# The first tile of v loaded by SyncE's queue behind f instead of by GpSimd's queue behind q and k of the second quad

## The chip, the cores and the metric

The kernel runs on one core of a Trainium2 chip. The metric is the device time of one execution in microseconds (us); the times of a kernel are given as the median of its runs. Profiles are of one execution each and have a time of their own.

## What is computed

The reference is causal attention with a forgetting decay, followed by an MLP with tanh-GELU. There are 8 batches of 8 heads, 576 positions and 64 columns per head; the MLP has 4608 tokens (8 x 576), a width of 512 and a hidden width of 2048. All inputs and the output are float32.

```python
log_f = np.log(np.clip(f, 0.0001, 1.0))
cum = np.cumsum(log_f, axis=-1)
scores = q @ k.T / sqrt(64) + cum[..., :, None] - cum[..., None, :]
attn = softmax(where(causal, scores, -1e9))
x = (attn @ v), heads side by side          # 4608 x 512
out = gelu_tanh(x @ w_in) @ w_out           # 4608 x 512
```

## The kernel before

The 64 heads are worked through as 16 quads of 4 heads (two quads per batch), and the 4608 tokens of the MLP as 9 chunks of 512. Per quad, k and q arrive as float32 and are cast to bf16 by the DMA (`load_one`, L204, issued from GpSimd, called POOL here), are transposed in 32x32 words by VectorE (DVE, L212) into kT and qT, and TensorE (PE) makes the scores (L275). ScalarE (ACT) takes their exponential into pt (L283), POOL or DVE set the part above the diagonal to zero (L289, L319). The decay does not enter the scores: as exp(cum_i - cum_j) falls apart into two factors, the key's factor wT = exp(-cum - 64) is multiplied into v (`make_vw`, L229, giving vw), and the query's factor cancels in the division by the denominator. The denominators are products of pt with w_bf, the bf16 copy of wT (L690, L691); the attention output is a product of pt with vw (L331 in the first two quads, L345 after), divided on its way into xT (L377). The MLP's first product (L414 for the first chunk, L390 and L463 after), GELU (L421, L398, L476) and second product (L609 for the first chunk, L542 after) follow, in part by a scheme with seven products for eight.

v comes per batch in five tiles of up to 128 positions, each for 8 heads: a tile is 128 x 8 x 64 float32, 256 KB, in runs of 64 values (L183). `load_v` takes the issuing engine as an argument. The word LP loads a tile of batch 0 by POOL's queue, LU the same by SyncE's (SP's) queue, LC and LX tiles of batch 1 by POOL's, LV and LB those of later batches by SP's.

The order of the work on every engine is the order in which it is written down: `setup()` and then tables of words, each word a function and its arguments (`ops`, L696; `run`, L747). A word such as `TK.0` issues its instructions on their engines at that place; engines then go on by themselves and wait for each other through semaphores. So POOL's DMA issues stand in one line with its memsets, masks and products. Two things hold back a DMA issue: data that it overwrites, and a semaphore that it shares with the eighth DMA before it from the same kind of queue, whose landing it waits for.

Around the change the order is this. In `setup()`, SP issues f; POOL issues k and q of quad 0, makes the identity, issues k and q of quad 1, makes the triangle. DVE clears buffers and clips f; ACT takes its logarithm; PE transposes it (L642). Then the words of SETUP: in the kernel before `TK.0` (DVE transposes k of quad 0) and `LP.0 LP.1` (POOL issues v tiles 0 and 1 of batch 0). After them the table FRONT begins:

```
Z TQ.0 LP.2 TR WI.1 TQ.1 S.0.0 B.1.384 CW WI.0 TK.1 S.0.2 LP.4 LP.3 B.2.256 vw.0.0 B.4.256 H.1.0.1 ...
```

Z are memsets on POOL (L649 to L652); TQ.0, TQ.1 and TK.1 the other transposes; WI pieces of w_in by POOL's queue; S.0.0 the scores of quad 0 for its first 256 positions; B matmuls that only keep PE busy (L254); CW the matmuls of the cumulated decay (L661, L663) with the exponential into wT (L666); `vw.0.0` the first use of v: DVE multiplies tiles 0 and 1, four heads, by wT (L229). `H.1.0.1` are scores of quad 1. Later words of FRONT, all on POOL, are q and k of quad 2, the rest of w_in, four pieces of w_out (WO, L199, 512 KB each) and the tiles of batch 1. The first chunk's second product (L609) needs all four pieces of w_out.

Of the kernel before, what the change touches and what calls it, by code (L numbers as in the profile page):

```python
# [16 lines left out]
def kernel(  # L17
# [51 lines left out]
    ON_ACT = ()  # L69

    SETUP = """
        TK.0 LP.0 LP.1
    """

    FRONT = """
# [723 lines left out]
```

## Time and profile before

| What | Value |
|---|---|
| Median of 3 runs | 326.88 us (326.15 to 329.17) |
| The profiled execution, its own time | 327.29 us |
| Span of its profile, first to last instruction | 325.6 us |
| DVE, ACT, POOL busy | 232.9, 207.3, 106.2 us |
| POOL's DMA queue (q0): packets, MB | 9632, 15.99 |
| SP's DMA queue (q1): packets, MB | 37664, 16.60 |
| HBM read, written | 36.85 MB, 9.44 MB |

The profile is read thus. PE is TensorE's matmuls, PEld its weight loads, which lie beside the matmuls. Lines such as L229 are lines of the kernel. "out<-in" names the tiles written and read. Idle time in square brackets is that of the engine just ahead of the instruction, with what ended it; "issue" is time in which the profile shows no releaser. A DMA's time to landing runs from its issue to the semaphore that tells of it. q0 is the queue of POOL (software_dynamic), q1 that of SP (hardware_dynamic); the core's 16 DMA engines serve both, and a share is the time that a queue's packets took, as a share of 16 engines' time, which can be over 100% as packets overlap. The small packets of 4 bytes, counted as "under 512 B" beside larger ones in q0, carry no data.

### The profile page before, as it was taken

To read this page: it belongs to the slowest core of one execution; us is meant where nothing else is said; L and a number is where in the kernel's file an instruction comes from. 1 tells how busy PE (TensorE), PEld (TensorE's weight loads), DVE (VectorE), ACT (ScalarE), POOL (GpSimd) and SP (SyncE) were. 2 spreads that over 40 slices of the span, in tenths; PEclk is the share of its full clock that TensorE was granted. 3 is DMA by queue.
4 is the path that set the end of the run, shared out by engine and by line. 5 is a ranking of instruction groups with operands and counts; after the bars stand their busy time and mean duration, and the time that the engine had idled before them with its cause. 6 is when DMAs were issued, how large, how long until landed. Compare 5 with 4: busy or idle time off the path is not lost.

```text
span 325.6 us, 12168 instructions
## 1 busy us (share of the span) xinstructions
PE 312.2 (96%) x5514; PEld 217.5 (67%) x5514; DVE 232.9 (72%) x374; ACT 207.3 (64%) x252; POOL 106.2 (33%) x145
## 2 busy tenths in 40 slices
PE   0999989999999999999999999999999999999996
PEld 0656834454777567766778887657765777588785
DVE  4665208898989886797769776778665865498674
ACT  4685656875856776579558765876668742746510
POOL 8879316442111215530643144403450150000000
PEclk9999999999999999999999999999999999999999
DMA  7999999586125961296119711761020102010212
GB/s 126 234 170 164 207 238 215 126 166 120 34 40 118 238 128 54 67 201 109 52 45 200 132 54 36 171 97 52 14 92 0 34 6 99 0 34 0 99 35 97
DMA packets 47492, 33.44 MB, mean 103 GB/s; under 512 B 29776, under 2 KB 42192, under 8 KB 47440
## 3 DMA queue, kind: packets, MB, share of 16 engines
q0 software_dynamic: 9632, 15.99, 28.4%
q1 hardware_dynamic: 37664, 16.60, 19.6%
q8 instruction: 43, 0.70, 0.9%
q10 hardware_dynamic: 144, 0.07, 0.1%
q14 instruction: 9, 0.07, 0.1%
HBM read 36.85 MB, written 9.44 MB: 142 GB/s over the span
## 4 chain that ended last, share of the span: by engine, by line
PE 83%; DMA 6%; POOL 5%; ACT 2%; DVE 1%; issue 1%; POOLq 0%; DVEq 0%
PE ps_w L542 29%; PE ps_h L390 25%; PE po L345 9%; PE ps_u L463 8%; PE ps_s L275 7%; DMA w_out_sb<-in_moe_w_out_dram 4%; PE pso L609 4%; ACT pt L283 2%; DMA q_c<-in_q_dram 2%; POOL pt L289 1%; POOL vw L229 1%; POOL w_out_sb L199 1%; POOL v_nat L183 1%; POOL w_in_sb L195 1%; PE cum_ps L663 1%
## 5 line engine op out<-in xcount | busy, mean ns | idle before, releaser
L283 ACT ACTIVATE pt<-ps_s 128x1024 bf16<-128x1024 f32 (+2 forms) x100 | 93.8, 988 | 48.8 <-PE ps_s L275 45.6
L390 PE MATMUL ps_h<-xT,w_in_sb 128*128 128x512 bf16 (+1 forms) x416 | 84.8, 354 | 0.1
L289 POOL TENSOR_SCALAR_AFFINE_SELECT pt<-pt 128x512 bf16<-128x512 bf16 (+3 forms) x65 | 39.7, 622 | 108.8 <-ACT pt L283 108.0
L390 PEld LDWEIGHTS <-w_in_sb 128*128 128x128 bf16 x416 | 40.6, 98 | 33.6 <-issue 0.4
L398 ACT ACTIVATE gT<-ps_h 128x1024 bf16<-128x1024 f32 x44 | 44.8, 1017 | 21.9 <-PE ps_h L390 21.6
L542 PEld LDWEIGHTS <-gT 128*32 128x32 bf16 (+1 forms) x1354 | 45.0, 97 | 3.8 <-issue 0.4
L542 PE MATMUL ps_w<-w_out_sb,gT 128*32 128x256 bf16 (+1 forms) x954 | 41.8, 273 | 0.0
L275 PE MATMUL ps_s<-qT,kT 32*128 32x64 bf16 (+5 forms) x896 | 36.6, 263 | 3.3 <-DVE qT L212 3.0
L542 PEld LDWEIGHTS <-gsum 128*32 128x32 bf16 (+1 forms) x1026 | 35.6, 97 | 3.0 <-issue 1.3
L229 POOL TENSOR_TENSOR vw<-v_nat,wT 128x1280 bf16<-128x1280 f32 (+1 forms) x13 | 29.4, 2262 | 11.4 <-DMA v_nat<-in_v_dram 11.4
L275 PEld LDWEIGHTS <-kT 32*128 32x128 bf16 x896 | 16.9, 93 | 19.5 <-issue 11.8
L542 PE MATMUL ps_w<-usum,gsum 128*32 128x256 bf16 (+1 forms) x791 | 29.3, 273 | 0.0
L377 DVE TENSOR_TENSOR xT<-po,rb 128x576 bf16<-128x576 f32 x26 | 19.7, 756 | 10.8 <-PE po L345 10.1
L559 DVE COPY snap<-ps_w 128x512 f32<-128x512 f32 x32 | 21.7, 677 | 6.7 <-PE ps_w L542 6.7
L479 DVE TENSOR_TENSOR usnap<-ps_u,usnap 128x512 f32<-128x512 f32 x27 | 17.8, 685 | 10.4 <-PE ps_u L463 6.1
L212 DVE STREAM_TRANSPOSE kT<-k_c 128x576 f32<-128x576 f32 x16 | 20.0, 1247 | 5.0 <-DMA k_c<-in_k_dram 5.0
L345 PE MATMUL po<-pt,vw 128*32 128x64 bf16 (+4 forms) x624 | 22.5, 279 | 0.0
L520 DVE TENSOR_TENSOR gsum<-gT 128x1024 bf16<-128x1024 bf16 x14 | 11.0, 785 | 14.8 <-ACT gT L476 12.7
L212 DVE STREAM_TRANSPOSE qT<-q_c 128x576 f32<-128x576 f32 x16 | 19.9, 1244 | 2.3 <-DMA q_c<-in_q_dram 2.1
L345 PEld LDWEIGHTS <-vw 128*32 128x32 bf16 x672 | 14.4, 97 | 10.4 <-issue 3.7
L206 POOL DMA_DIRECT2D k_c<-in_k_dram x16 | 9.1, 569 | 28.3 <-DVE kT L212 11.6
L476 ACT ACTIVATE gT<-usnap 128x512 bf16<-128x512 f32 x18 | 11.1, 630 | 9.5 <-DVE usnap L479 9.5
(113 smaller groups left out, 431.5 us busy)
## 6 DMA issues: line engine op xcount, KB each, us to landing
out_dram<-o_st SPq DMA_DIRECT2D x35, 256.0 KB, 2.3
k_c<-in_k_dram POOLq DMA_DIRECT2D x16, 288.0 KB, 5.5
q_c<-in_q_dram POOLq DMA_DIRECT2D x16, 288.0 KB, 5.9
v_nat<-in_v_dram SPq DMA_DIRECT2D x16, 256.0 KB, 4.6
v_nat<-in_v_dram SPq DMA_DIRECT2D x20, 128.0 KB, 3.9
v_nat<-in_v_dram POOLq DMA_DIRECT2D x8, 256.0 KB, 8.4
w_in_sb<-in_moe_w_in_dram POOLq DMA_DIRECT2D x8, 256.0 KB, 7.8
w_out_sb<-in_moe_w_out_dram POOLq DMA_DIRECT2D x4, 512.0 KB, 11.9
```

The source lines that it names most:

```text
L212: return nc.vector.transpose(out=dst.rearrange("p s c -> p (s c)").bitcast(FP32) .rearrange("p (t a) -> p a t", a=S // 32), in_=src.rearra ...
L229: return eng.tensor_mul(vw[i % 2][:, t0:t1], vb[:, t0:t1, h0:h0 + 4, :], wT[:, i, t0:t1, :].unsqueeze(3).to_broadcast([128, t1 - t0, 4, D]))
L275: nc.tensor.matmul(tiles[h // 2][:, h % 2, c0:c0 + nq], key_columns(i, key, h, c), qq[32 * h:32 * h + 32, q0:q0 + nq, c], start=(c == 0 an ...
L283: nc.scalar.activation(p[:, 2 * g:2 * g + 2, off:off + n], t[:, :, 0:n], AF.Exp, scale=scale)
L289: nc.gpsimd.affine_select(out=x, in_=x, compare_op=ALU.is_ge, fill=0.0, base=0, pattern=pattern, channel_multiplier=-1)
L345: nc.tensor.matmul(po[r0:r0 + w.shape[-1], 448 + q0:448 + q0 + nq], w, p[:, h, col:col + nq], start=(key in (0, "low")), stop=(key in ("lo ...
L377: nc.vector.tensor_mul(xT[:, 2 * u + x, r0 + s0:r0 + s1], po, rbs[i, part])
L390: nc.tensor.matmul(ph[:, j, n * cols:(n + 1) * cols], w_in_sb[:, dt, 128 * ft:128 * ft + 128], xT[:, dt, h0:h0 + cols], start=(dt == 0 and ...
L398: nc.scalar.activation(gelus(c, 2 * pr, 2), ph, AF.Gelu_apprx_tanh)
L463: nc.tensor.matmul(ps[:, n, :], w[:, d, 128 * n:128 * n + 128], x[:, d, :], start=(first and n == 0 and d == 0), stop=(d == 1), skip_group ...
L542: nc.tensor.matmul(ps[c0:c0 + width, n, cols[0]:cols[1]], x[:, j, 128 * n + c0:128 * n + c0 + width], w[:, j, cols[0]:cols[1]], start=(fir ...
L559: copy(kept[name], ps)
```

## The change

In SETUP the word `LP.0` is gone from behind `TK.0`, and `LU.0` stands ahead of it. Both words load the same tile: v of batch 0, positions 0 to 127, all 8 heads, into the first tile of v_nat0.

```diff
     SETUP = """
-        TK.0 LP.0 LP.1
+        LU.0 TK.0 LP.1
     """
```

The two words differ only in the engine that issues the DMA:

```python
"LU": lambda t: load_v(0, ts=(t,)),                    # eng=nc.sync
"LP": lambda t: load_v(0, ts=(t,), eng=nc.gpsimd),
```

In the order of the instructions by engine, SP has one DMA more, directly behind that of f and ahead of its first output; POOL has one fewer, the first of its two v tiles behind q and k of quad 1. PE, DVE and ACT have the same instructions in the same order.

## The prediction

> **What bounds the kernel now.** I read, in this order, the page's busy shares, the chain of waits that ended last, the timeline of the first 62 us, and the DMA view of short windows.
>
> ```profile
> span 325.6 us, 12168 instructions
> ...
> PE 312.2 (96%) x5514; PEld 217.5 (67%) x5514; DVE 232.9 (72%) x374; ACT 207.3 (64%) x252; POOL 106.2 (33%) x145
> ```
>
> TensorE (PE) is busy for 312.2 of 325.6 us. So a change can gain or lose only in the 13.4 us in which PE is idle, or by lengthening them. By the timeline 7.9 of these lie before 8.65 us (4.91 before the first matmul at 4.91, 2.97 before L275). After 46.2 us the list of PE's waits for other work adds up to 0.9 us, of which 0.6 is the wait that ends at 46.13. So the first 46 us decide. The chain of waits in that stretch (start, length, what):
>
> ```profile
> 2.02 5.29 DMA q_c<-in_q_dram
> ...
> 8.65 0.83 PE ps_s L275 x14
> ...
> 31.97 14.11 DMA w_out_sb<-in_moe_w_out_dram
> 46.09 0.04 issue
> 46.13 1.67 PE pso L609 x7
> ```
>
> The reader is to see two transfers on it: q of quad 0, which lands at 7.31 and lets DVE make qT and PE start its scores at 8.65; and the last quarter of w_out, which lands at 46.08. The timeline has the waits that matter here (start, duration, engine, line, then idle time and releaser):
>
> ```profile
> 11.32 1.26 DVE L212 STREAM_TRANSPOSE qT<-q_c 128x576 f32<-128x576 f32 x1 [1.95 <-DMA q_c<-in_q_dram]
> ...
> 13.84 0.09 PEld L275 LDWEIGHTS <-kT 32*128 32x128 bf16 x1 [0.21 <-DVE kT L212]
> ...
> 42.90 1.02 PE L609 MATMUL pso<-w_out_sb,gT 128*128 128x512 bf16 x4 [0.63 <-DMA w_out_sb<-in_moe_w_out_dram]
> ...
> 46.13 1.67 PE L609 MATMUL pso<-w_out_sb,gT 128*128 128x512 bf16 x7 [0.61 <-DMA w_out_sb<-in_moe_w_out_dram]
> ```
>
> First: q of quad 1 is awaited by DVE for 1.95 us and, through its transposes, by PE for 0.21. Last: PE waits for w_out 0.63 and 0.61, together 1.24 us. A PE that comes to 42 us later, while w_out lands as before, finds these waits shorter. No row shows PE or DVE waiting for the first tile of v.
>
> **The change part by part.** The edit takes one DMA (256 KB, L183) out of GpSimd's (POOL's) queue, where it is the fifth, and puts it second into SP's. The order of the instructions on PE, DVE and ACT is the same in both programs.
>
> *POOL.* The removed issue is half of the "x2" group at 4.70 (1.82 us), so 0.91 us. What follows moves up by 0.91: the memsets of L649 from 6.56 to 5.65, the next v tile from 8.19 to 7.28, the first two w_in pieces from 9.10 to 8.19. POOL's next wait for ACT with idle time is L289 at 17.24 (1.84 idle), so the lead ends there and is no gain by itself. Each POOL DMA waits for the landing of the eighth before it; with one DMA gone the pairs from the thirteenth on are the same as before. The four pairs ahead of that (two w_in pieces, two v tiles) wait for a transfer one place earlier, which lands sooner. Cost nothing.
>
> *SP.* The new issue stands behind f's (0.58 us at 0.81) and ahead of nothing until SP's first output at 47.91. f's own packets are ahead of v's; f lands at 3.6 and its use, cum_ps at 9.70, has over 3 us of slack. Cost nothing.
>
> *The 16 DMA engines.* Here is the price. v's packets now run while k and q of quad 0 are under way. I price this by rows of the same two queues in the steady part, where SP's queue brings v tiles beside POOL's q and k:
>
> ```profile
> q0 software_dynamic: 527, 1.10, 95.8%
> q1 hardware_dynamic: 608, 0.15, 16.1%
> ```
> ```profile
> q0 software_dynamic: 200, 0.43, 108.6%
> ```
>
> The columns are packets, MB and share of 16 engines. The first fence is the window 112 to 118 us, both queues full: 527 packets of q0 in 6 us are 88 per us, beside 1.15 packets of v for each of q0. The second is 46 to 48, q0 alone: 100 per us. So company costs q0 14%. One v packet takes 16.1% x 6 us x 16 / 608 = 25 ns of an engine. In the window 3 to 6.3 q0 has 266 packets and 103% of the engines, almost all of k and q of quad 0. 14% of 3.3 us is 0.45 us: q lands at 7.76, and L275 starts at 9.1. Lower end: the windows 2 to 3 and 3 to 4 have the engines at 0.72 and 0.91, so 0.37 us could take v for nothing, which leaves 0.1. Upper end: all of v served first. From 109 to 110 us, with q1 alone, 1039 such packets passed in 1 us, so v's 1024 take 1.0; the far row is 52 to 58 us, with outputs too, where q0 made 349 packets in 6 us, 58 per us, which would make 3.3 us into 5.7, +2.4. I take 0.45: the row 112 to 118 has the same two kinds of transfer and no stores. Nothing is gained at q's landing, since no packet that went ahead of it is removed.
>
> [...] The windows show 1.15 to 1, so I keep the row.
>
> *The second quad.* Per engine k and q of both quads are 32 packets; beside them go 32 x 1.15 = 37 of v, 37 x 25 ns = 0.9 us. So q of quad 1 and the transposes at 11.32 and 12.42 come up to 0.9 later, kT at 14.55 instead of 13.65. PE, itself 0.45 late, could absorb about 0.2 (it goes on at 14.10 where kT had come at 13.65 and the weight load at 13.84), so its scores of quad 1 are late by 0.7. ACT, which runs without a gap from 13.36 to 22.36, gets a gap of 0.3 there. I carry 0.7; ends 0.1 and 1.3.
>
> *v itself.* The tile landed 7.8 us after 4.70, at 12.5, and the next at 13.6, just before L229 used both at 13.71 (wT, its other input, came at 13.46). Now the second is first in POOL's queue and lands near 12.6. The first has 27 of 64 packets per engine left when q of quad 1 is through; it lands near 13 to 14. L229 waits for kT until 14.55 anyway, so cost nothing. If that cover is gone, the casts of L690 behind it are late next; they ended at 15.04 and the first product that reads w_bf began at 16.24, so the first 1.2 us are free.
>
> *From 14 to 46 us.* PE is busy without a gap over 0.2 until 31.3, so 0.7 arrives there in full. The w_out pieces decide what is left of it. POOL's issues after 17.24 follow ACT, so they move by 0.7 too. But transfers are late by less if the engines have a backlog:
>
> ```profile
> q0 software_dynamic: 196, 0.18, 74.3%
> ```
> ```profile
> DMA packets 126, 0.21 MB, mean 141 GB/s; under 512 B 7, under 2 KB 56, under 8 KB 126
> ```
>
> The first is 19.5 to 21 us: engines run dry, for the next issue (q, 19.78) came late. The second is 21 to 22.5: 56 - 7 = 49 packets of w_in are still moving, so the slowest engines had not run dry when the new packets came, and a transfer has landed only when its last engine is done. From 23 to 46 the queue's share is 112%. So w_out is late by something between -0.9 (the tile's 256 KB gone from ahead of it at the 285 GB/s of 9 to 11 us) and +0.7 (POOL's delay in full). I take +0.2: near zero for the backlog, above it for the 74.3%.
>
> *Sum.* PE reaches 42.27 0.7 late; its two waits for w_out shrink by 0.7 - 0.2 = 0.5 of their 1.24; 0.2 us is left. Nothing after 46.2 gives or takes. The profiled execution took 327.29 us (span 325.6 and 1.69 around it), 0.41 above the median of the three runs, 326.88. So 327.5 for that execution, and 327.1 for the median. Its own range is -0.2 to +0.7: 326.7 to 327.6.
>
> **The rivals.**
>
> *Nothing is absorbed.* w_out is late by as much as PE, for POOL's issues hang on ACT. For it: POOL waits for ACT at 17.24 and again at 24.65 (0.94 idle). Against: 49 packets of backlog. +0.7 to +1.3: 327.6 to 328.2.
>
> *v goes first, and it is slower.* Place: the engines from 3 us on. Price: 1.0 us at q's landing, up to 2.4 by the row 52 to 58. For it: from 111 to 112, when q0 began beside a full q1, q0 passed 21 packets and q1 425. Against: 112 to 118. It decides from the point where q's delay is over the 1.24 us that the w_out waits can take up, or where these move along; +1.1 to +2.1: 328.0 to 329.0. [...]
>
> *w_out lands earlier, and it is faster.* The engines use the half-empty time at 2 to 4 us for v, and 256 KB fewer stand ahead of w_out. Then both waits of 1.24 go, less what PE is late: -0.5, and -1.2 if q is not late at all: 325.7 to 326.4. Against: 103% and 112% shares leave little empty time, and POOL's later issues wait for ACT.
>
> That v comes too late for L229 is within the second rival's sum. That the change does nothing to any transfer is within my own range.
>
> **How the numbers follow.** Chances: absorbed 0.45, nothing absorbed 0.25, v first 0.12, earlier w_out 0.18. The likeliest gives 327.1. The range leaves out the far half of the faster case and the end of the slower one, and allows for a median of few runs where three runs of one kernel spread from 326.15 to 329.17: 326.0 to 328.8. About 1% (3.3 us) is what a measurement of this kernel can tell from no change. Faster by that much would need more than all of PE's waits at w_out: 0.01. Slower by that much needs 3.3 us at q's landing, or v first at the far row's price with nothing absorbed and more: 0.03. Within 1%: 0.96.
>
> **What would show it.** In the changed kernel's timeline: the POOL group at 4.70 is one issue and L649 starts near 5.65; the first qT starts near 7.8 instead of 7.33 and L275 near 9.1; the second qT near 12.0; L229 on DVE near 14.5 with no wait for v; L609's waits for w_out together near 0.7 instead of 1.24, the last ending near 46.3. I am wrong if L275 starts after 10 (v went first), at 8.65 (company is free), if L229 waits for v, or if the last w_out wait ends before 45.8 or after 46.9.

## The result and the profile after

| | Kernel before | Changed kernel |
|---|---|---|
| Median, 22 runs each | 326.81 us (325.48 to 329.17) | 327.94 us (326.98 to 330.22) |
| Ratio to before, 95% interval | | 1.0032 (1.0018 to 1.0046) |
| The profiled execution | 327.29 us | 328.84 us |
| Span | 325.6 us | 327.1 us |

The changed kernel is slower by 1.13 us, 0.3%: less than the 1% that a few runs can tell, but with 22 runs the interval lies above 1. (A ratio is recorded with its interval for each comparison; it is not the quotient of the two medians.) Its page begins as follows.

```profile
span 327.1 us, 12153 instructions
...
PE 312.1 (95%) x5499; PEld 217.8 (67%) x5514; DVE 233.5 (71%) x374; ACT 207.3 (63%) x252; POOL 104.8 (32%) x144
```

PE's busy time over the whole span is the same (312.1 against 312.2 us), but this profile has 15 matmul records fewer (5499 against 5514), most of them late in the span. What counts here is the stretch up to the end of PE's last wait for w_out, at 46.13 in the kernel before and at 47.36 in the changed one. One row for each (stretch, its length, then busy time and instructions of PE, PEld, DVE, ACT and POOL, granted clock, DMA share, GB/s):

```profile
0.00:46.13 46.13, 36.01 (x473) 24.91 (x474) 21.33 (x46) 29.21 (x36) 31.07 (x53) 1.00 1.05 189
```
```profile
0.00:47.36 47.36, 36.87 (x471) 25.34 (x473) 20.88 (x46) 29.24 (x36) 30.22 (x52) 1.00 1.00 184
```

Of the 1.23 us by which this moment is later, PE is busy for 0.86 and idle for 0.37: its matmuls take longer, and it also waits longer. The chain of waits in the first 60 us (start, length, what) shows where the first part comes in and what it has become at 47 us:

```profile
2.03 6.21 DMA q_c<-in_q_dram
...
9.57 0.83 PE ps_s L275 x13
...
11.90 2.35 PE cum_ps L663 x8
...
33.55 13.77 DMA w_out_sb<-in_moe_w_out_dram
47.32 0.04 issue
47.36 1.67 PE pso L609 x7
```

q of quad 0 lands 6.21 us after its issue instead of 5.29, and PE starts at 9.57 instead of 8.65. The eight matmuls of L663, which are no different, then take 2.35 us instead of 1.79. The last piece of w_out is used at 47.36 instead of 46.13. The same steps in the timeline of the changed kernel (start, duration, engine, line; idle time and releaser last):

```profile
8.26 1.26 DVE L212 STREAM_TRANSPOSE qT<-q_c 128x576 f32<-128x576 f32 x1 [0.42 <-DMA q_c<-in_q_dram]
...
11.36 1.26 DVE L212 STREAM_TRANSPOSE qT<-q_c 128x576 f32<-128x576 f32 x1 [1.37 <-DMA q_c<-in_q_dram]
...
14.79 0.69 DVE L229 TENSOR_TENSOR vw<-v_nat,wT 128x512 bf16<-128x512 f32 x1 [1.10 <-ACT wT L666]
14.84 1.24 PE L254 MATMUL idle_ps<-idle 128*128 128x256 bf16 x6
...
16.01 0.97 PE L275 MATMUL ps_s<-qT,kT 32*128 32x256 bf16 x16
...
19.08 1.22 POOL L289 TENSOR_SCALAR_AFFINE_SELECT pt<-pt 128x512 bf16<-128x512 bf16 x2 [4.38 <-ACT pt L283]
...
21.60 0.57 POOL L206 DMA_DIRECT2D q_c<-in_q_dram  x1
...
44.10 1.02 PE L609 MATMUL pso<-w_out_sb,gT 128*128 128x512 bf16 x4 [0.74 <-DMA w_out_sb<-in_moe_w_out_dram]
...
47.36 1.67 PE L609 MATMUL pso<-w_out_sb,gT 128*128 128x512 bf16 x7 [0.64 <-DMA w_out_sb<-in_moe_w_out_dram]
```

The reader is to see the lateness grow to 1.91 us and arrive at w_out as 1.23: q's transpose at 8.26 (before 7.33, +0.93); the scores of quad 1 at 16.01 (before 14.10, +1.91); POOL, which has 4.38 us idle for ACT where it had 1.84, issues q of quad 2 at 21.60 (before 19.78, +1.82); and PE's two waits for w_out are 0.74 and 0.64, no shorter than before (0.63 and 0.61). The 0.68 made up between 16.01 and 47.36 is not made up there; 0.57 of it is idle time ahead of L414 at 31.86 in the kernel before, which is gone in the changed one. q of quad 1 (11.36, before 11.32) is not late, and DVE's use of v waits for wT and not for v.

What the DMA engines do at the start is in the DMA view, with packets, MB and share of 16 engines. First the window 3 to 4 us, the kernel before, then the changed one.

```profile
q0 software_dynamic: 57, 0.13, 91.5%
```
```profile
q1 hardware_dynamic: 259, 0.07, 28.6%
q0 software_dynamic: 14, 0.03, 27.8%
```

While v's 256-byte packets pass, POOL's queue gets 14 packets through where it had 57, and both queues together fill only 56% of the engines' time: here POOL's queue hardly starts, and not because the engines are full. Then the window 5 to 6 us, in the same order.

```profile
q0 software_dynamic: 97, 0.20, 110.7%
```
```profile
q1 hardware_dynamic: 392, 0.10, 48.5%
q0 software_dynamic: 63, 0.11, 63.3%
```

Here the two queues together are at 112%, and POOL's queue loses packets to v all the same: 63 instead of 97, with 6.2 of v for each. Over 2 to 6 us POOL's queue passes 149 packets instead of 257; 56 of these 108 are lost before 4 us, 52 after it. So q's transfer is late both because it hardly starts and because it shares full engines later.

### The profile page after: what moved, and what is told of

Its sections match the earlier page's. It is cut to its first block, busy times and chain, and to the rows that moved or that the text cites. A ratio compares the mean times of both kernels' runs of the same rounds, so it can differ in the third digit from the quotient of the medians.

```text
span 327.1 us, 12153 instructions
## 1 busy us (share of the span) xinstructions
PE 312.1 (95%) x5499; PEld 217.8 (67%) x5514; DVE 233.5 (71%) x374; ACT 207.3 (63%) x252; POOL 104.8 (32%) x144
## 4 chain that ended last, share of the span: by engine, by line
PE 81%; DMA 6%; POOL 5%; DVE 3%; issue 2%; ACT 2%; POOLq 0%; DVEq 0%
PE ps_w L542 29%; PE ps_h L390 23%; PE po L345 9%; PE ps_u L463 8%; PE ps_s L275 8%; DMA w_out_sb<-in_moe_w_out_dram 4%; PE pso L609 4%; DMA q_c<-in_q_dram 2%; ACT pt L283 1%; POOL pt L289 1%; POOL vw L229 1%; DVE gsum L520 1%; PE cum_ps L663 1%; POOL w_out_sb L199 1%; POOL w_in_sb L195 1%
## 5 line engine op out<-in xcount | busy, mean ns | idle before, releaser
L390 PE MATMUL ps_h<-xT,w_in_sb 128*128 128x512 bf16 (+1 forms) x403 | 83.9, 354 | 0.9 <-issue 0.2
L275 PE MATMUL ps_s<-qT,kT 32*128 32x64 bf16 (+5 forms) x896 | 36.7, 264 | 4.3 <-DVE qT L212 3.8
L229 POOL TENSOR_TENSOR vw<-v_nat,wT 128x1280 bf16<-128x1280 f32 (+1 forms) x13 | 29.4, 2261 | 12.6 <-DMA v_nat<-in_v_dram 12.6
L275 PEld LDWEIGHTS <-kT 32*128 32x128 bf16 x896 | 16.9, 93 | 20.8 <-issue 12.2
L345 PE MATMUL po<-pt,vw 128*32 128x64 bf16 (+4 forms) x624 | 22.5, 278 | 0.0
L520 DVE TENSOR_TENSOR gsum<-gT 128x1024 bf16<-128x1024 bf16 x14 | 11.8, 845 | 14.8 <-ACT gT L476 12.7
L609 PE MATMUL pso<-w_out_sb,gT 128*32 128x512 bf16 (+1 forms) x140 | 15.6, 380 | 1.6 <-DMA w_out_sb<-in_moe_w_out_dram 1.4
```

The source lines that it names most:

```text
L229: return eng.tensor_mul(vw[i % 2][:, t0:t1], vb[:, t0:t1, h0:h0 + 4, :], wT[:, i, t0:t1, :].unsqueeze(3).to_broadcast([128, t1 - t0, 4, D]))
L275: nc.tensor.matmul(tiles[h // 2][:, h % 2, c0:c0 + nq], key_columns(i, key, h, c), qq[32 * h:32 * h + 32, q0:q0 + nq, c], start=(c == 0 an ...
L345: nc.tensor.matmul(po[r0:r0 + w.shape[-1], 448 + q0:448 + q0 + nq], w, p[:, h, col:col + nq], start=(key in (0, "low")), stop=(key in ("lo ...
L390: nc.tensor.matmul(ph[:, j, n * cols:(n + 1) * cols], w_in_sb[:, dt, 128 * ft:128 * ft + 128], xT[:, dt, h0:h0 + cols], start=(dt == 0 and ...
L609: nc.tensor.matmul(pso[c0:c0 + cols, :], gT[:, ft, 128 * n + c0:128 * n + c0 + cols], w_out_sb[:, ft, :], start=(ft == 0), stop=(ft == N_F ...
```

## The experiments

The theories: **v ahead**, SP's tile holds up k and q of quad 0, and that lateness is the cost; **clock**, the late start of PE makes its matmuls fast later still, and this is most of the cost (in the first profiles the eight of L663 took 1.79 and 2.35 us, and quad 1 began 5.45 and 6.44 us after L275; by this difference of 0.99 a "step" in an expectation is to be read); **issue**, POOL's late issue of the next transfers, which hangs on ACT, carries the lateness to w_out, so that the waits there take up nothing; against **bytes**, w_out lands when the engines have moved everything ahead of it. A kernel was timed beside the kernel before on the same chip, and each has one profiled execution of its own, which is not its median. By "fast" and "slow" matmuls I mean how long matmuls of one shape take in the trace; the profiles' granted clock reads 1.00 in every microsecond from 5 to 18 in both kernels, so the name "clock" is an interpretation that no row shows.

**The two kernels once more.** No edit.

> The kernel before, profiled once more, nothing changed. In its first profile the small filler matmuls of L254 with 256 columns that begin at 13.08 took 273 ns each, and the 128x256 products of L663 380; in the changed kernel's profile the same two took 421 and 634, until 15.7. [...]

> The changed kernel, profiled once more and timed beside the kernel before, nothing changed. Both theories: the first qT at 8.2 to 8.3, L275 at 9.5 to 9.6, ratio 1.002 to 1.005. [...] Theory 'transfers alone': the scores of quad 1 at 16.0 again.

The kernel before: 326.44 us, qT at 6.92, L275 at 8.24, scores of quad 1 at 13.76. The changed kernel: 327.44 us, ratio 1.0029 (1.0011 to 1.0047); qT at 8.88, L275 at 10.19, scores of quad 1 at 16.63. q's landing differs from one execution to the next by 0.4 to 0.6 us in either kernel, so single profiles must be compared with care; the change stands out from that. The stretch from L275 to quad 1 was 5.52 us and 6.44 us, as in the first pair (5.45 and 6.44). Four profiles do not tell whether this is the kernels' or chance. The second changed execution missed the expectation: q was later than 8.2 to 8.3, and quad 1 later than 16.0. Both profiled executions of the changed kernel (328.84 and 328.63 us) are the third longest of their runs, 0.90 and 1.19 us above the medians, so they show more lateness than a median execution has.

**The tile beside the rest, without relief for POOL** (kernel before, one more transfer; its values are not used).

```diff
+        nc.sync.dma_start(out=v_nat[1][:, 0, :, :], in_=v[0, :, 0:128, :].rearrange("h p d -> p h d"))
         run(SETUP)
```

> The kernel before, with one transfer more: SP loads the same 256 KB of v behind f into the first tile of the second v buffer, which is loaded again later, so the result of it is not used; POOL's queue keeps its own v tile. Theory 'v ahead of k and q of quad 0': the first qT at 8.2 to 8.3 and L275 at 9.5 as in the changed kernel, ratio 1.002 to 1.006. Theory 'it is the tile that is missing on POOL's side' (the order or the shared semaphores of its issues): L275 at 8.65 to 8.9 and ratio under 1.001.

Measured 327.61 us, ratio 1.0020 (1.0000 to 1.0040). The timeline of this kernel:

```profile
8.37 1.26 DVE L212 STREAM_TRANSPOSE qT<-q_c 128x576 f32<-128x576 f32 x1 [0.94 <-DMA q_c<-in_q_dram]
9.69 0.83 PE L275 MATMUL ps_s<-qT,kT 32*128 32x256 bf16 x16 [3.91 <-DVE qT L212]
...
13.94 0.83 PE L254 MATMUL idle_ps<-idle 128*128 128x256 bf16 x6
...
14.95 1.22 PE L275 MATMUL ps_s<-qT,kT 32*128 32x256 bf16 x16 [0.19 <-ACT pt L283]
```

POOL's queue is as before, and q is late all the same: SP's transfer does it. But here the six fillers take 0.83 us, where they took 1.24 in the changed kernel, and quad 1 starts 5.26 us after L275. So the slow matmuls do not follow from a late L275 alone: this one was later than the 9.57 of the changed kernel's first profile. Further on, the timeline of this execution has at L609:

```profile
42.08 1.89 PE L609 MATMUL pso<-w_out_sb,gT 128*128 128x512 bf16 x7
44.53 2.66 PE L609 MATMUL pso<-w_out_sb,gT 128*128 128x512 bf16 x11
```

No wait for w_out is left: it landed at 45.5, 24.8 us after POOL's issue of q of quad 2 at 20.63, and PE came late enough not to notice. So in this execution, the shortest of the twelve at 326.85 us, the waits did take up lateness, as the prediction had it; the median of this kernel is 0.81 above before all the same.

**Half the tile.** In the changed kernel, heads 0 to 3 by SP, heads 4 to 7 by POOL.

```diff
-        LU.0 TK.0 LP.1
+        LH.0 LT.0 TK.0 LP.1
...
+        "LH": lambda t: load_v(0, 0, 4, ts=(t,)),
+        "LT": lambda t: load_v(0, 4, 4, ts=(t,), eng=nc.gpsimd),
```

> Half of the change: heads 0 to 3 of the tile (128 KB) by SP behind f, heads 4 to 7 by POOL where they were. Theory 'v ahead of k and q, price by size': the first qT at 7.7 to 7.9 and L275 at 9.0 to 9.2. [...] Theory 'a fixed start-up cost of the second queue': the first qT at 8.2 or later, as with the whole tile.

Measured 327.49 us, ratio 1.0004 (0.9981 to 1.0028), qT at 7.75, L275 at 9.07, quad 1 at 15.09. The five profiles with a whole tile on SP have q transposed at 8.07 to 8.99, mean 8.51; the five with none there and DVE's order unchanged at 6.86 to 7.33, mean 7.08. The half is at 0.67 of a full 1.43, which speaks for a price by size and against a fixed one of a second queue; with a scatter of 0.4 to 0.6 between executions, one profile of the half does not show it. The time does not decide: the medians are 0.56 us apart (326.93 before), but the interval of the ratio goes from below 1 to 1.0028.

**SP waits until q of quad 0 has landed.** Again in the changed kernel.

```diff
-        LU.0 TK.0 LP.1
+        LU.0@LQ.0 TK.0 LP.1
```

> The changed kernel, with SP's v tile held back until q of quad 0 has landed; POOL's queue stays relieved of the tile. Theory 'v ahead of k and q of quad 0': the first qT is back at 7.3 and L275 at 8.65, and the time is that of the kernel before, 326.5 to 327.1 us, ratio 0.998 to 1.001. Theory 'the tile is better off in POOL's queue at any time' (its small packets slow k and q of quad 1 and the w_in pieces): L275 at 8.65, but the time stays 0.5 us or more above before.

Measured 327.67 us (326.31 to 334.24), ratio 1.0023 (0.9993 to 1.0053): unclear. The 0.87 us above before (326.80) would fit the second theory's "0.5 us or more", but the interval includes no change, and four of the twelve executions took 331.19 to 334.24 us. The profiled one is among them (331.77 us); I read only its waits:

```profile
8.98 0.83 PE L275 MATMUL ps_s<-qT,kT 32*128 32x256 bf16 x16 [3.31 <-DVE qT L212]
...
17.13 0.69 DVE L229 TENSOR_TENSOR vw<-v_nat,wT 128x512 bf16<-128x512 f32 x1 [3.34 <-DMA v_nat<-in_v_dram]
...
18.55 0.35 PE L331 MATMUL po_m<-pt,w_bf 128*32 128x256 bf16 x8 [2.06 <-DVE w_bf L690]
```

L275 is nearly back (q lands at 7.6), but the tile, issued at 7.67, comes so late that DVE waits 3.34 us for it, and through the casts behind it PE 2.06. So in this execution one wait was exchanged for another, which neither theory had named: the tile on SP was early and in q's way without the hold, and late for L229 with it.

**A late L275 with no transfer changed.** On DVE, the casts of the masks stand ahead of the first qT.

```diff
-        Z TQ.0 LP.2 TR WI.1 TQ.1 S.0.0
+        Z TR TQ.0 LP.2 WI.1 TQ.1 S.0.0
```

> The kernel before with one reordering on DVE alone: the casts of L656 and L657 stand ahead of the first qT, so that qT and L275 come about 0.7 us later (9.3) while no transfer is changed. [...] Theory 'transfers': without v beside k, q and w_in the 0.7 is taken up by the waits for w_out at L609 (1.24 in the kernel before), and the time is that of before within 0.3 us.

> The reordering on DVE alone once more (casts of L656 and L657 ahead of the first qT, no transfer changed), for a profile of it. Theory 'POOL's issue sets w_out': qT at 8.0, L275 at 9.1 to 9.4; q of quad 2 is issued by POOL 0.7 to 1.8 us after the 19.78 of the kernel before, the larger number if the matmuls get fast a step later; the last w_out wait ends 25 to 26.3 us after that issue; the time is 0.4 to 1.0 us above before. Theory 'the tile's bytes set w_out': the last w_out wait ends at 45.2 to 46.2 as before, and the time is within 0.3 us of before.

The first run: 327.58 us beside 326.93, ratio 1.0021 (1.0006 to 1.0036); the execution profiled took 1793 us and is not used. The second: 327.39 beside 326.89, ratio 1.0022 (0.9999 to 1.0044). So 0.5 to 0.65 us by the medians for the 0.7 of DVE's work, with the transfers untouched: lateness of L275 alone reaches the end. How much of it does is less sure, as the intervals are 0.2 to 1.2 us and 0.0 to 1.4 us. The theory that the waits for w_out take it all up ("transfers" in the first expectation, "bytes" in the second) had less than 0.3 and is not borne out. The second's profile missed its expectation: q happened to land at 6.7, so that qT stood at 7.31 and L275 at 8.63; its last w_out wait ended at 45.04, 25.05 us after POOL's issue at 19.99, which the issue theory had named.

**Fillers ahead of L275**, in the kernel before (the edit below) and in the changed one (`LU.0 TK.0 LP.1 B.14.256`).

```diff
-        TK.0 LP.0 LP.1
+        TK.0 LP.0 LP.1 B.14.256
```

> The kernel before with 14 more filler matmuls (L254, 256 columns) on PE between the transposes of L642 and the first scores, where PE is idle for 3 us. Nothing waits for them. Theory 'clock': matmuls are fast at or soon after L275, the stretch from L275 to the first scores of quad 1 falls from 5.45 us to 4.0 to 4.6, and the time falls by 0 to 1.0 us, depending on the waits for w_out. Theory 'transfers alone': no change of that stretch by more than 0.3 us.

> The changed kernel with the same 14 filler matmuls. Theory 'clock': L275 stays at 9.5 or later, but the stretch to the scores of quad 1 falls from 6.44 us to 4.0 to 5.3, the waits for w_out take up the rest, and the time comes to 326.4 to 327.0 us, within 0.4 us of the same fillers without the change. Theory 'transfers alone' (v's tile costs what it delays): it stays 0.8 to 1.2 us above the kernel before with fillers.

Measured 326.01 us, ratio 0.9980 (0.9958 to 1.0002), and 327.09 us, ratio 1.0010 (0.9985 to 1.0034): 1.08 apart, where the clock theory had 0.4 at most and the other 0.8 to 1.2. The timelines of L275 and of the scores of quad 1, without the change and with it:

```profile
8.58 0.52 PE L275 MATMUL ps_s<-qT,kT 32*128 32x256 bf16 x16 [0.20 <-DVE qT L212]
...
13.31 0.97 PE L275 MATMUL ps_s<-qT,kT 32*128 32x256 bf16 x16 [1.04 <-DVE kT L212]
```
```profile
9.38 0.52 PE L275 MATMUL ps_s<-qT,kT 32*128 32x256 bf16 x16 [0.47 <-DVE qT L212]
...
13.42 1.06 PE L275 MATMUL ps_s<-qT,kT 32*128 32x256 bf16 x16 [0.35 <-DVE kT L212]
```

The fillers do make L275 fast (0.52 us for 16, not 0.83), and the stretch to quad 1 falls to 4.04 us in the changed kernel; without the change it is 4.73, as PE now waits 1.04 for k of quad 1. So how long the matmuls stay slow moves by what PE did before, but the difference between the medians stays. Each of the two intervals is about 1.5 us wide, so this speaks against the clock as the main cause and does not exclude a part. In this pair of profiles POOL issues q of quad 2 at 18.90 and 19.01, yet the last w_out wait ends at 45.52 with the change, and there is none without it: w_out landed 24.6 and 26.5 us after the issue. Why those differ is open; the two intervals overlap as well.

**Two POOL issues moved up**, in the kernel before and in the changed one: q of quad 2 and a w_in piece ahead of the masks that wait for ACT.

```diff
-        WI.5 H.1.0.0 D.0.0
+        WI.5 LQ.2 WI.4 H.1.0.0 D.0.0
...
-        M.0.1 LQ.2 V.0.1.0 B.1.256 H.1.1.0 D.1.0 WI.4 H.0.3.0
+        M.0.1 V.0.1.0 B.1.256 H.1.1.0 D.1.0 H.0.3.0
```

> The kernel before with two POOL issues moved up: q of quad 2 and one w_in piece are issued directly behind the w_in pieces at 14 us, ahead of the masks that wait for ACT at 17.24. Theory 'POOL's issue sets w_out': the engines do not run dry at 20 us, the last wait for w_out ends about 1 to 2 us earlier than 46.13 or is gone, time 325.5 to 326.5 us. Theory 'the engines' total of bytes sets w_out': no change of the last wait by more than 0.4 us, time 326.6 to 327.2.

> The changed kernel with the same two issues moved up. Theory 'POOL's issue sets w_out': w_out no longer moves with the late ACT, the waits at L609 are short, and what is left of the difference to the same kernel without the change is PE's own lateness, 0.3 to 1.8 us, no longer taken up by any wait; time 326.5 to 327.8. Theory 'total of bytes': 327.5 to 328 as without the move.

Measured 325.55 us, ratio 0.9953 (0.9935 to 0.9970), the fastest kernel of the study, and 326.63 us, ratio 0.9985 (0.9969 to 1.0002). Both times lie in the ranges of the issue theory and outside those of the other. The timeline without the change, then with it:

```profile
15.40 0.57 POOL L206 DMA_DIRECT2D q_c<-in_q_dram  x1
...
44.58 1.67 PE L609 MATMUL pso<-w_out_sb,gT 128*128 128x512 bf16 x7 [0.39 <-DMA w_out_sb<-in_moe_w_out_dram]
```
```profile
10.30 0.83 PE L275 MATMUL ps_s<-qT,kT 32*128 32x256 bf16 x16 [4.33 <-DVE qT L212]
...
15.43 0.57 POOL L206 DMA_DIRECT2D q_c<-in_q_dram  x1
...
44.93 2.55 PE L609 MATMUL pso<-w_out_sb,gT 128*128 128x512 bf16 x11
```

With the change no wait for w_out is left at L609, as PE is the later of the two; the kernels are still 1.08 us apart. In these two executions L275 is at 8.18 and 10.30, L609 begins at 40.71 and 42.47 (1.76 apart), and the times are 325.84 and 327.62 (1.78 apart). The stretch from L275 to quad 1 is 6.11 and 5.76, so slow matmuls are not behind the difference in this pair; PE's late start is. One sentence of the issue theory did not hold: w_out still moves with the change, landing at 44.5 and 45.8, though POOL issues q of quad 2 at the same time in both. POOL's first issue of w_out itself, which comes after further masks, is at 27.86 and 29.63.

**Both together**, fillers and early issues, in the kernel before.

> The kernel before with both: the 14 fillers ahead of the first scores and the two issues moved up. If the clock and w_out are the two things that hold back the first 46 us, this is the fastest of all: 324.5 to 325.8 us. If the fillers' gain is lost in the wait for k of quad 1 (1.04 us in the kernel with fillers alone), it equals the better of the two alone, 325.5 to 326.2.

Measured 325.68 us, ratio 0.9972 (0.9949 to 0.9996): no better than the early issues alone, the second of the two outcomes, though it lies in the range of the first as well. Its L275 took 0.82 us for 16 in spite of the fillers, so these do not make it fast in every execution.

The profiled executions side by side (us):

| Kernel | qT of quad 0 | L275 | quad 1 | q of quad 2 issued | last w_out wait ends | time |
|---|---|---|---|---|---|---|
| before | 7.33 | 8.65 | 14.10 | 19.78 | 46.13 | 327.29 |
| before, again | 6.92 | 8.24 | 13.76 | 19.44 | 45.25 | 326.44 |
| changed | 8.26 | 9.57 | 16.01 | 21.60 | 47.36 | 328.84 |
| changed, again | 8.88 | 10.19 | 16.63 | 22.23 | 47.32 | 328.63 |
| tile beside the rest | 8.37 | 9.69 | 14.95 | 20.63 | none (landed 45.5) | 326.85 |
| half the tile | 7.75 | 9.07 | 15.09 | 20.77 | 45.57 | 326.75 |
| casts first, again | 7.31 | 8.63 | 14.31 | 19.99 | 45.04 | 326.26 |
| before, fillers | 7.27 | 8.58 | 13.31 | 18.90 | none (landed 43.5) | 325.31 |
| changed, fillers | 8.07 | 9.38 | 13.42 | 19.01 | 45.52 | 326.62 |
| before, early issues | 6.86 | 8.18 | 14.29 | 15.40 | 44.58 | 325.84 |
| changed, early issues | 8.99 | 10.30 | 16.06 | 15.43 | none (landed 45.8) | 327.62 |
| before, both | 7.04 | 8.62 | 13.56 | 15.30 | 44.16 | 325.34 |

In every row with a wait, the time less the end of the last w_out wait is 281.1 to 281.5 us. So the differences between these executions, all but 0.4 us, are made before that moment. In the seven such rows with POOL's order unchanged it comes 24.8 to 26.5 us after POOL issues q of quad 2; in the two without a wait w_out landed 24.6 and 24.8 us after it. This scatter of 1.9 us is as large as the 1.8 to 2.8 us by which POOL issues later in the changed kernel's two profiles than in the two of the kernel before, so a single landing cannot be forecast from the issue.

## Why the prediction was right, and where its steps were not

The forecast of a change within 1% was right, and 327.94 lies in the range; 327.1, the likeliest, was 0.84 too low. But the account given the best chance (0.45) is not the one that the changed kernel's profiles show, and 327.94 lies above that account's own range of 326.7 to 327.6: that the time lies in the range is owed to the width given to the rivals, not to that account. What these profiles show is two of the rivals together: most of v goes ahead of q (chance 0.12; its 328.0 to 329.0 is just above the median), and nothing is absorbed at w_out (0.25; 327.6 to 328.2). Two signs that the prediction gave for being wrong came: the last w_out wait ended after 46.9 (47.36 and 47.32), and in the second profile L275 started after 10 (10.19).

- *Only PE's idle time can gain or lose*: incomplete. Of the 1.23 us by which the last w_out wait ends later in the first profile, 0.86 is PE's busy time, as matmuls of one shape did not always take the same time (the six fillers ahead of quad 1 took 0.83 us before and 1.24 in the changed kernel).
- *POOL's lead is no gain, and SP has nothing behind it*: right. POOL's wait for ACT grew from 1.84 to 4.38 us. The wait for the eighth DMA before is in the trace of before as 0.23, 0.31, 1.91 and 2.79 us of POOL's idle time, ahead of its issues at 31.97, 33.04, 36.73 and 40.84, and not earlier. f landed 2.8 us after its issue in both kernels.
- *q's landing*: the mis-sized term. I took 0.45 from the window 112 to 118, with 1.15 packets of v for each of POOL's; it was 0.93 in the first profile and 1.43 as a mean of five against five. From 3 to 6.3 us POOL's queue passed 172 packets instead of 266, beside 893 of v, which is 5.2 for each. The upper end of 1.0, all of v served first, was nearer, and the row that I gave for that rival, 111 to 112, where POOL's queue began beside a full SP queue, was the nearer case for the first microseconds. By what rule the engines divide themselves between the two queues is not shown: 3 to 4 us has 28.6% and 27.8%, engines half empty; on full engines there were 6.2 packets of v for each of POOL's from 5 to 6 us, but 1.6 (112 to 72) from 4 to 5.
- *The second quad*: wrong in the first profile. q of quad 1 came 0.04 late and not 0.9, as most of v had passed by then; as a mean of the same five against five it was 0.55 late. PE's lateness at quad 1 was 1.91 for another reason: 0.92 from L275 and 0.99 because the matmuls between stayed slow longer.
- *The clock*: not foreseen. The trace of before had it, in fillers of 272 to 283 ns from 13.08 on. In the changed kernel's first profile most of those from 14.84 on took 394 to 421 ns. From L275 to quad 1 the executions of the table without fillers took 5.26 to 6.44 us, so single ones differ by up to 1.18 there. The pairs with fillers and with early issues, both still 1.08 apart, speak against the clock as the main cause of the median's 1.13; a share of it is not excluded.
- *v itself*: right. It was early enough for L229, and the kernel that holds it back showed the wait that comes when it is not.
- *w_out is late by 0.2 only*: the step that failed. It was late by 1.23, and the two waits were 1.38 together instead of 0.74. I had inferred a backlog from 49 packets between 21 and 22.5 us; the view gives the 16 engines together, so that the slowest of them still had work is not shown. In the changed kernel that window reads:

```profile
q0 software_dynamic: 21, 0.02, 7.3%
```

  The share is 7.3% (0.9% in its second profile) where the kernel before had 108.7% (102.2%): the engines had run dry, since POOL's next issue had moved from 19.78 to 21.60. What PE's lateness was absorbed in was the 0.57 us ahead of L414 at 31.86. With the two issues moved up, the window is full in both kernels (115.1% and 112.0%); the kernel before is 1.34 us faster for it, and the changed one comes to 326.63 from 327.94 and 327.44 in its earlier comparisons. That fits the issue theory; it does not make the two kernels equal.

Shown by experiments: that SP's tile makes q late, with or without relief for POOL; that lateness of L275 alone costs time, with no transfer changed; that issuing two transfers ahead of POOL's masks gains 1.3 us in the kernel before. Only argued: that w_out's landing, through POOL's late issues, is what keeps the lateness from being absorbed in the median execution, as it was absorbed in one profile (the tile beside the rest); and why POOL's queue hardly starts beside SP's. Open: what makes w_out's landing vary from 24.6 to 26.5 us after the issue, and what share the slow matmuls have in the 1.13.

## What to carry to other kernels

A transfer put on a second, idle queue is not free because its own user has time (here q landed 6.21 us after its issue instead of 5.29): ask which transfer on the first queue is just starting and who waits for that one. Before trusting a later wait to absorb a delay, look whether the transfer behind that wait is issued by an engine that will be late too. In a kernel with so little idle time, a gain was to be had not by another queue but by issuing what was ready ahead of a wait: two issues moved up gave 0.5%.

## What the runs showed of the hardware that was not expected

From 3 to 4 us, with SP's queue at 259 small packets, POOL's queue passed 14 instead of 57 while the engines were half empty; in the stretch from 112 to 118 us of the kernel before, with both queues under way, the two had shared the engines with POOL's queue at 95.8%. Nor is the ratio fixed once both run: 1.6 packets of SP's for each of POOL's from 4 to 5 us of the changed kernel, 6.2 from 5 to 6. A price read in one stretch did not hold in another.

The moment at which matmuls become fast is not fixed to the start of PE's work. Without fillers, the stretch from L275 to quad 1 took, among others, 5.26 us (L275 at 9.69), 5.45 (8.65), 6.02 (9.07), 6.11 (8.18) and 6.44 (9.57 and 10.19). What sets this moment no run shows: the granted clock reads 1.00 from 5 to 18 us in the first profiles of both kernels.
